# One tile's output product moved a few steps back in a hand-written order, in a retention and phase-MLP kernel on one core

## The chip, the core and the metric

The kernel runs as one program on one core of a Trainium2 chip. The metric is device microseconds of one launch. Five engines run side by side and meet only at semaphores: PE (matrix products; its weight loads are listed apart as PEld), DVE, ACT and POOL (elementwise work), and SP, which here only issues DMAs. Each engine takes its own instructions strictly in the order in which the program emits them, so an instruction that waits holds up all that is behind it on that engine.

## The reference

Two stages follow each other. The first is a retention recurrence over batch 4, 8 heads, 768 positions and head size 64:

```python
gamma = 1.0 - 2.0 ** (-5.0 - np.arange(H))
for t in range(S):
    state = gamma * state + einsum('bhd,bhe->bhde', k[:, :, t], v[:, :, t])
    y[:, :, t] = scale * einsum('bhd,bhde->bhe', q[:, :, t], state)
```

Its output, with the heads side by side (x is 4 x 768 x 512), goes through a phase MLP:

```python
theta = x @ w_theta
zr, zi = x * cos(theta), x * sin(theta)
y = einsum('ts,bsd->btd', w_tok_r, zr) + einsum('ts,bsd->btd', w_tok_i, zi)
u = x + y
out = u + maximum(u @ w_ch, 0)
```

## The kernel before, in words

The 768 positions of a batch are six tiles of 128, so there are 24 tiles, numbered 0 to 23. Retention works on 24 units (a batch, 256 positions, half of the heads), also numbered 0 to 23; units 22 and 23 give the two halves of tiles 22 and 23, units 20 and 21 those of tiles 20 and 21.

There is no scheduler. The list `ORDER` (lines 23 to 87) names every step as a token, and the last lines of the kernel run one small function per token, in that order. A token `M.16.3` calls `M(16, 3)`; a last letter v, a, p or s names the engine or the queue (DVE, ACT, POOL, SP). The place of a token in the list therefore sets the place of its instructions on each engine that it uses, and nothing else does. The tokens that matter below:

- `I.n` (line 457) is the state product of unit n: four PE matmuls of the block-diagonal state `sbd` with the queries. `SB.n.g` (line 140 or 138) copies the state into `sbd` before it, and `S0.n` (line 437) updates the state on DVE.
- `Y.n`, `ST.n` and `A.n` (lines 469, 419 and 392) are the other three retention products, 16 small PE matmuls each. `m.n` (line 401) masks what `A.n` gave, on DVE, for `Y.n`. `XA.n.c` (line 487) and `XB.n.c` (line 140 or 138) write the halves of the finished tile `xT`.
- `Ht.C` and `Hh.C` (line 518) are the theta product of tile C, four PE matmuls of 512 columns; `CT.C.w` and `CN.C.w` (line 525) take cosine and sine on ACT, and `z.C` (line 532) multiplies by x.
- `M.t.s` (line 563) is one sixth of the token sum of output tile t: two PE matmuls of 512 columns. `u.t` (line 570) adds x on DVE.
- `Du.t` (line 585) transposes u into `uT` with a DMA from SP; `Dx.C` (line 508) and `Dk.n` (line 374) do the same for x and for queries and keys.
- `Ot.t` and `O.t` (line 593) are the output product of tile t, four PE matmuls of 512 columns on `uT`. `ft.t` and `f.t` (line 599) add u and the rectified product on DVE; `SO.t` stores it.
- `Vs.*` (line 633) and `ta`, `tb`, `tc_` (lines 646 to 653) prepare sums and differences for the last batch, whose token sums `Na`, `Nb`, `Nc` (line 681) use fewer products.

`Ht` and `Ot` take their PSUM from the same two banks (tag "tr"); `M`, `Hh` and `O` take theirs from two others (tag "acc"). `uT` has three buffers and `ot` four.

Constants are allocated in the order in which the functions `const2`, `const1`, `constQ` and so on run. `qsc`, the decay factors of the queries, is 2 x 12 x 2 floats, so 192 bytes of each partition.

Of the kernel before, what the change touches and what calls it, by code (L numbers as in the profile page):

```python
# [15 lines left out]
FT = mybir.dt.float32  # L16
# [52 lines left out]
SB.20.0.a M.14.3 M.14.2 CT.18.0 CT.18.1 I.20 Lq.23.s M.14.5 A.21 u.13 Dk.22 cv.21.p Y.20 ck.23.a Vs.2.1.v  # L69
z.18.v ST.21 S0.21.v Ot.9 SB.21.0.p cv.22.p Ht.19 M.15.5 SB.21.1.a u.14 m.21 M.15.3 M.15.0 XB.20.1.a cq.23.p  # L70
S1.21 Lv.23.s M.16.0 Dx.19 XB.20.0.v ft.9 Du.12 I.21 A.22 Y.21 ST.22 CT.19.1 cv.23.p SO.6.a XA.21.1 M.15.1
CT.19.0 M.15.2 S0.22.v XA.21.0 m.22 SB.22.0.a SB.22.1.a M.15.4 Vs.0.1.p Ot.12 u.15 Ht.21 I.22 M.16.3 CT.21.0
ta.18.v CT.21.1 M.16.5 z.19.v Y.22 ft.12 Dk.23 ST.23 XB.22.1.a S0.23.v A.23 Du.13 Hh.20 Du.14 Dx.20 M.16.4
Ot.13 Vs.1.1.v XB.22.0.a ta.19.p CN.20.0 m.23 CN.20.1 Vs.2.0.v Ot.14 Dx.21 SB.23.0.p Vs.3.1.v SB.23.1.a
tb.19.p I.23 z.21.v M.16.2 Y.23 M.17.2 M.17.0 M.16.1 M.17.4 ft.13 XA.23.0 XA.23.1 Dx.22 Ht.22 Dx.23 u.16
z.20.v Na.9.1 CT.22.0 CT.22.1 ta.21.v Hh.23 CN.23.0 Du.15 M.17.3 ta.20.v M.17.1 tb.18.v Na.9.0 tb.20.p
Na.10.2 Na.10.1 tc_.20.v tb.21.v z.22.v Na.10.0 CN.23.1 SO.9.a M.17.5 Na.9.3 z.23.v ta.22.v tb.22.v ta.23.v
SO.13.a tc_.18.v Na.10.3 Du.16 Na.10.4 tb.23.v Na.9.2 tc_.23.p Na.9.4 Na.9.5 Na.10.5 u.17 c1.9 g1.9 Ot.15
O.16 e5.9 cx.9.p Du.17 SO.12.s SO.8.a c1.10 g1.10 ft.15 gx.9.p Nb.9.0 e5.10 Nb.9.2 ex.9.v Nb.9.5 Nb.9.1
Nb.9.3 Nb.9.4 f.16 Nb.10.1 tc_.19.v uc.9 Nb.10.3 ub.9 Ot.17 Nb.10.5 Nb.10.4 tc_.22.p ex.10.v ua.9 Nc.9.0  # L80
gx.10.p Na.11.4 Nb.10.2 Nb.10.0 Nc.9.5 cx.10.v tc_.21.p Na.11.1 ft.14 Nc.9.3 ft.17 Nc.9.4 Na.11.3 uc.10
Nc.9.1 Nc.9.2 Na.11.5 Du.18 ub.10 ud.9 Na.11.2 Na.11.0 Nc.10.1 Nc.10.2 SO.15.a Nc.10.5 c1.11 ua.10 e5.11
Nc.10.3 g1.11 O.18 f.18 SO.17.s Nc.10.0 Du.21 gx.11.v Du.19 SO.14.a Nc.10.4 Nb.11.1 SO.16.s ud.10 Nb.11.3
Nb.11.5 Nb.11.2 ex.11.v Nb.11.4 Nb.11.0 ub.11 O.21 ua.11 f.21 uc.11 Tu.20 O.19 Du.22 Nc.11.4 SO.18.s Nc.11.3
Nc.11.2 Eu.20.v Nc.11.1 cx.11.v Nc.11.0 Tuh.1 Nc.11.5 ud.11 SO.21.a O.22 Euh.1 Tuh.0 Euh.0 O.20 f.19 Oh.0
SO.19.s Oh.1 f.22 f.20 fh.0 SO.22.a SO.20.s fh.1 Z.31 SOh.1 SOh.0
""".split()


# [11 lines left out]
def kernel(  # L101
# [16 lines left out]
    P = 128  # L118
    nT = S // P
    nD = dm // P  # L120
    nI = nT // 2
# [6 lines left out]
    const = ctx.enter_context(tc.tile_pool(name="const", bufs=1))  # L128
# [64 lines left out]
    K = {}  # L193

    def const1():
        zero = const.tile([P, dm], BF, name="zero")
        nc.vector.memset(zero, 0.0)
        K["zero"] = zero
        K["sbd"] = [[const.tile([P, 2, 2, P], BF, name=f"sbd{h}{x}") for x in range(2)]
                    for h in range(2)]  # L200
        K["wth"] = const.tile([P, nD, dm], BF, name="wth")
        K["wch"] = const.tile([P, nD, dm], BF, name="wch")
        K["wT"] = [const.tile([P, nT, S], BF, name="wtr"),
                   const.tile([P, nT, S], BF, name="wti")]
        K["row"] = [[const.tile([P, hi - lo, S], BF, name=f"row{r}{lo}")
                     for lo, hi in groups] for r in range(2)]
# [58 lines left out]
                                 bias=K["lscale"], scale=K["lgp"][:, x:x + 1])  # L265

    def const3():
        K["qsc"] = const.tile([P, 2, nI * 4, 2], FT, name="qsc")
        K["vsc"] = const.tile([P, nI, 2, H], FT, name="vsc")
        nc.scalar.activation(K["vsc"].rearrange("p i a h -> p (i a) h"), K["arg"], AF.Exp,  # L270
                             bias=K["zerob"], scale=-1.0)
        K["qx"] = const.tile([P, H // 2, S], FT, name="qx")
# [501 lines left out]
    CT, ft = CN, f  # L774
# [32 lines left out]
```

## Time and profile before

| | |
|---|---|
| time, median of 3 runs | 165.76 us (165.52 to 166.09) |
| the profiled execution's own time | 166.06 us |
| its span, first to last instruction | 164.3 us |
| around the span | 1.76 us |
| granted TensorE clock, mean | 0.999 |

Busy time of the engines in the span: DVE 128.3 us, ACT 82.7 us, POOL 80.9 us; PE is discussed in the prediction. The view of stretches gives, for a window of time, how long each engine was busy; the view of waits gives for an instruction that sat idle what it waited for; the chain of waits follows the run back from its last instruction. In a timeline row the columns are start in us, length in us, engine, source line, operation, output<-input, size and count; brackets give the idle time before it and what ended it. Consecutive matmuls overlap, so the pace of PE is read from start to start and not from their lengths.

### The profile page before, as it was taken

The page shows a single profiled execution, that of the slowest core. Times are in us where ns is not written, and L with a number is a line of the kernel's source. Part 1 is how long each engine was busy: PE and PEld are TensorE (multiplying, and loading weights), DVE is VectorE, ACT ScalarE, POOL GpSimd, SP SyncE. Part 2 cuts the span into 40 slices and gives each one's busy share as a digit, 9 for nine tenths or more (in the row PEclk, how much of TensorE's full clock was granted, in tenths as well). Part 3 has the DMA queues.
Part 4 walks back from the last instruction along what each step waited for, and adds up shares of the span by engine and source line. Part 5 has one row for each costly group of instructions (what it writes and reads, how often), then busy time and mean ns, then how long its engine had stood idle before and what let it go on. Part 6 is the DMA issues. An engine that isn't in the chain of part 4 may idle for free.

```text
span 164.3 us, 5075 instructions
## 1 busy us (share of the span) xinstructions
PE 154.5 (94%) x2072; PEld 90.4 (55%) x2072; DVE 128.3 (78%) x254; ACT 82.7 (50%) x151; POOL 80.9 (49%) x115
## 2 busy tenths in 40 slices
PE   5997889999999999999999999999995999999992
PEld 1354655656666655654555565544552446678650
DVE  5499687977994895994779895887889688796782
ACT  4967798984657245772333724933641715100010
POOL 7797189087214823730307699939177501440000
PEclk9999999999999999999999999999999999999999
DMA  4999999999999998959999896999999306633846
GB/s 131 321 311 227 302 321 237 270 221 218 202 238 138 308 224 186 328 111 284 347 250 199 200 219 198 227 191 291 171 249 124 66 15 144 186 138 97 224 166 221
DMA packets 62919, 34.93 MB, mean 213 GB/s; under 512 B 26416, under 2 KB 59952, under 8 KB 62896
## 3 DMA queue, kind: packets, MB, share of 16 engines
q1 hardware_dynamic: 51680, 23.73, 67.1%
q10 hardware_dynamic: 8528, 7.47, 15.1%
q0 software_dynamic: 2688, 3.41, 12.1%
q8 instruction: 16, 0.26, 0.7%
q14 instruction: 7, 0.06, 0.1%
HBM read 25.69 MB, written 6.29 MB: 195 GB/s over the span
## 4 chain that ended last, share of the span: by engine, by line
PE 72%; DMA 9%; DVE 6%; POOL 5%; issue 3%; ACT 2%; SPq 0%; DVEq 0%; POOLq 0%
PE y_ps L563 26%; PE o_ps L593 11%; PE th_ps L518 9%; DMA row<-in_moe_w_tok_r_dram 6%; PE r_ps L469 3%; PE xw L681 3%; DMA uT<-u 3%; PE kq_ps L358 3%; PE xwv L681 3%; PE vv L681 2%; PE at_ps L392 2%; PE w_ps L540 2%; PE r_ps L457 2%; PE r_ps L419 1%; DVE kqb L344 1%
## 5 line engine op out<-in xcount | busy, mean ns | idle before, releaser
L563 PE MATMUL y_ps<-z,wtr 128*128 128x512 bf16 x108 | 41.0, 380 | 0.0
L563 PE MATMUL y_ps<-z,wti 128*128 128x512 bf16 x108 | 40.9, 379 | 0.0
L350 POOL TENSOR_TENSOR vb<-vf,vsc 128x512 bf16<-128x512 f32 x18 | 19.0, 1057 | 21.3 <-DMA vf<-in_v_dram 14.6
L401 DVE TENSOR_TENSOR at<-at_ps,mask 128x1024 bf16<-128x1024 f32 x24 | 29.2, 1216 | 0.1
L593 PE MATMUL o_ps<-wch,uT 128*128 128x512 bf16 x92 | 23.3, 380 | 1.7 <-DMA uT<-u 1.7
L518 PE MATMUL th_ps<-wth,xT 128*128 128x512 bf16 x96 | 24.7, 379 | 0.1
L525 ACT ACTIVATE cs<-th_ps,halfpi 128x512 bf16<-128x512 f32 x24 | 16.4, 685 | 12.9 <-PE th_ps L518 4.9
L532 POOL TENSOR_TENSOR z<-cs,x_sb 128x1024 bf16<-128x1024 bf16 x8 | 17.0, 2124 | 9.0 <-DVE z L532 4.7
L525 ACT ACTIVATE cs<-th_ps,zerob 128x512 bf16<-128x512 f32 x24 | 16.4, 684 | 7.6 <-PE th_ps L518 7.5
L138 ACT COPY kqT<-kq_ps 128x1024 bf16<-128x1024 bf16 x12 | 12.1, 1012 | 11.8 <-PE kq_ps L358 11.8
L140 POOL CAST sbd<-s 64x256 bf16<-64x256 f32 (+1 forms) x17 | 8.9, 525 | 18.3 <-DVE s L437 17.0
L570 DVE TENSOR_TENSOR u<-y_ps,x_sb 128x512 bf16<-128x512 f32 x18 | 12.4, 686 | 7.1 <-PE y_ps L563 6.9
L599 DVE SCALAR_TENSOR_TENSOR ot<-o_ps,u 128x512 f32<-128x512 f32 x23 | 15.6, 685 | 2.1 <-PE o_ps L593 2.1
L563 PEld LDWEIGHTS <-wtr 128*128 128x128 bf16 x108 | 10.5, 97 | 9.7
L563 PEld LDWEIGHTS <-wti 128*128 128x128 bf16 x108 | 10.6, 98 | 8.8 <-DVE wti L140 0.2
L593 PEld LDWEIGHTS <-uT 128*128 128x128 bf16 x92 | 8.3, 98 | 9.7 <-DMA uT<-u 2.2
L518 PEld LDWEIGHTS <-xT 128*128 128x128 bf16 x96 | 8.8, 98 | 8.3
L138 ACT CAST sbd<-s 64x256 bf16<-64x256 f32 (+1 forms) x24 | 8.9, 372 | 8.3 <-DVE s L437 6.5
L313 PE MATMUL zz<-zero 128*128 128x512 bf16 x30 | 10.3, 479 | 1.9 <-DVE part L232 1.9
L358 PE MATMUL kq_ps<-ident,kqb 128*128 128x128 bf16 x120 | 11.1, 220 | 0.9 <-ACT kqb L138 0.7
L532 DVE TENSOR_TENSOR z<-cs,x_sb 128x1024 bf16<-128x1024 bf16 x16 | 10.9, 686 | 1.1 <-DMA x_sb<-xT 0.9
L138 ACT CAST kqb<-kqf 128x512 bf16<-128x512 f32 x17 | 10.3, 620 | 2.2 <-DMA kqf<-in_k_dram 2.2
(127 smaller groups left out, 276.9 us busy)
## 6 DMA issues: line engine op xcount, KB each, us to landing
vf<-in_v_dram SPq DMA_DIRECT2D x20, 256.0 KB, 5.5
kqf<-in_k_dram SPq DMA_DIRECT2D x19, 256.0 KB, 5.0
kqf<-in_q_dram SPq DMA_DIRECT2D x17, 256.0 KB, 5.3
out_dram<-ot ACTq DMA_DIRECT2D x12, 256.0 KB, 3.1
out_dram<-ot SPq DMA_DIRECT2D x11, 256.0 KB, 3.7
kqf<-in_q_dram ACTq DMA_DIRECT2D x7, 256.0 KB, 5.0
kqf<-in_k_dram ACTq DMA_DIRECT2D x5, 256.0 KB, 5.8
vf<-in_v_dram ACTq DMA_DIRECT2D x4, 256.0 KB, 6.4
```

The source lines that it names most:

```text
L138: nc.scalar.copy(dst, src)
L350: engines[e].tensor_mul(in_blocks(vb), by_token(raw["vf", n]), _bcast_last(K["vsc"][:, i, :, h * HU:(h + 1) * HU], D))
L358: nc.tensor.transpose(st["kq_ps", n][:, 4 * w + x, :], st["kqb", n][:, w, x * P:(x + 1) * P], K["ident"])
L401: nc.vector.tensor_mul(at.rearrange("p g j a t -> p (g j) (a t)"), st["at_ps", n].rearrange("p g j a t -> p (g j) (a t)"), _bcast_mid(K["m ...
L518: nc.tensor.matmul(th_ps, st["xT", C][:, j, :], K["wth"][:, j, :], start=(j == 0), stop=(j == 3))
L525: nc.scalar.activation(st["cs", C][:, w, :], st["th_ps", C], AF.Sin, bias=K["zerob" if w else "halfpi"], scale=1.0)
L532: engines[e].tensor_mul(st["z", b][:, c], st["cs", C], _bcast_mid(x_of(C), 2))
L563: nc.tensor.matmul(st["y", t], K["wT"][r][:, s0, t0 * P:(t0 + 1) * P], st["z", b][:, s0, r, :], start=(done == 0 and r == 0), stop=(done = ...
L570: nc.vector.tensor_add(st["u", t], st["y", t], st["x", b][:, t0, :])
L593: nc.tensor.matmul(o_ps, st["uT", t][:, j, :], K["wch"][:, j, :], start=(j == 0), stop=(j == nD - 1))
L599: nc.vector.scalar_tensor_tensor(st["ot", t], st["o", t], 0.0, st["u", t], ALU.max, ALU.add)
L681: nc.tensor.matmul(o, a, m_, start=(phase == 0 and n == 0 and k != 1), stop=n == nT - 1, skip_group_check=True)
```

## The change

Two tokens are put elsewhere in `ORDER`, and one allocation is made earlier. `Ot.12` stood ahead of `u.15`; it now stands behind `M.16.5`, so behind `Ht.21`, `I.22`, `M.16.3` and `M.16.5`. `ft.12` stood behind `Y.22`; it now stands between `z.19.v` and `Y.22`.

```diff
-... M.15.4 Vs.0.1.p Ot.12 u.15 Ht.21 I.22 M.16.3 CT.21.0
-ta.18.v CT.21.1 M.16.5 z.19.v Y.22 ft.12 Dk.23 ST.23 ...
+... M.15.4 Vs.0.1.p u.15 Ht.21 I.22 M.16.3 CT.21.0
+ta.18.v CT.21.1 M.16.5 Ot.12 z.19.v ft.12 Y.22 Dk.23 ST.23 ...
...
     def const1():
+        K["qsc"] = const.tile([P, 2, nI * 4, 2], FT, name="qsc")
         zero = const.tile([P, dm], BF, name="zero")
...
     def const3():
-        K["qsc"] = const.tile([P, 2, nI * 4, 2], FT, name="qsc")
         K["vsc"] = const.tile([P, nI, 2, H], FT, name="vsc")
```

On PE, behind the last matmul of `M.15.4` (the line 563 row at the top), these are the first rows of each step up to `Y.22` (line 469). A name with a number behind it after "waits" is a semaphore: DMAHW is a DMA's, the others an engine's. Before:

```order
L563 MATMUL y_ps<-z,wti 128x512
L593 LDWEIGHTS uT [waits DMAHW7_49]
L593 MATMUL o_ps<-wch,uT 128x512 [waits DVE_49]
...
L518 LDWEIGHTS xT
L518 MATMUL th_ps<-wth,xT 128x512 [waits Activation_49]
...
L457 LDWEIGHTS sbd_96 [waits DVE_49,Activation_49]
...
L563 MATMUL y_ps<-z,wtr 128x512
...
L469 MATMUL r_ps<-at,vb 64x128 [waits DVE_49]
```

And now, from the same row on:

```order
L563 MATMUL y_ps<-z,wti 128x512
L518 LDWEIGHTS xT
L518 MATMUL th_ps<-wth,xT 128x512 [waits DVE_49]
...
L518 LDWEIGHTS xT [waits DVE_49]
...
L457 LDWEIGHTS sbd_97 [waits DVE_49,Activation_49]
...
L563 MATMUL y_ps<-z,wtr 128x512
...
L593 LDWEIGHTS uT [waits DMAHW7_49]
L593 MATMUL o_ps<-wch,uT 128x512
...
L469 MATMUL r_ps<-at,vb 64x128 [waits DVE_49]
```

The eight instructions of `Ot.12` stand behind 24 others that were behind them. `Ht.21` now takes the PSUM bank that `ft.9` read last (a wait on DVE), and `Ot.12` the one that `CT.19` read last.

On DVE, from `u.15` (line 570) over `ta.18`, `z.19` and `ft.12` (line 599) to `S0.23` (line 437), `Vs.1.1` (line 633) and `m.23` (line 401), the rows of the change are:

```order
L570 TENSOR_TENSOR u<-y_ps,x_sb 128x512 [waits DMAHW2_49,DVE_49,PE_49]
L646 TENSOR_TENSOR zs<-z 128x512
L532 TENSOR_TENSOR z<-cs,x_sb 128x1024 [waits DMAHW6_49,Activation_49]
L599 SCALAR_TENSOR_TENSOR ot<-o_ps,u 128x512 [waits DMAHW2_49,PE_49]
L437 TENSOR_TENSOR s_2780<-r_ps,s_2780 128x128 [waits PE_49]
L633 TENSOR_TENSOR row_109<-row_106,wtr 128x1536 [waits DMASW5_49,Pool_49]
L401 TENSOR_TENSOR at<-at_ps,mask 128x1024 [waits PE_49]
```

Nothing moved there: before, the same rows stand in the same order (`Y.22`, past which `ft.12` was written, has no DVE instruction). ACT, POOL and SP keep their order too. The earlier `qsc` puts every constant from `zero` to `mask` (the states `sbd`, the weights `wth`, `wch`, `wtr`, `wti` and their raw rows among them) 192 bytes further along in its partition and adds no instruction.

More of the change, by code (lines that the diff above doesn't have):

```diff
@@ L71 @@
 S1.21 Lv.23.s M.16.0 Dx.19 XB.20.0.v ft.9 Du.12 I.21 A.22 Y.21 ST.22 CT.19.1 cv.23.p SO.6.a XA.21.1 M.15.1
[L72 to L85, printed above, removed]
@@ L86 @@
-SO.19.s Oh.1 f.22 f.20 fh.0 SO.22.a SO.20.s fh.1 Z.31 SOh.1 SOh.0
+CT.19.0 M.15.2 S0.22.v XA.21.0 m.22 SB.22.0.a SB.22.1.a M.15.4 Vs.0.1.p u.15 Ht.21 I.22 M.16.3 CT.21.0
+ta.18.v CT.21.1 M.16.5 Ot.12 z.19.v ft.12 Y.22 Dk.23 ST.23 XB.22.1.a S0.23.v A.23 Du.13 Hh.20 Du.14 Dx.20
+M.16.4 Ot.13 Vs.1.1.v XB.22.0.a ta.19.p CN.20.0 m.23 CN.20.1 Vs.2.0.v Ot.14 Dx.21 SB.23.0.p Vs.3.1.v
+SB.23.1.a tb.19.p I.23 z.21.v M.16.2 Y.23 M.17.2 M.17.0 M.16.1 M.17.4 ft.13 XA.23.0 XA.23.1 Dx.22 Ht.22
+Dx.23 u.16 z.20.v Na.9.1 CT.22.0 CT.22.1 ta.21.v Hh.23 CN.23.0 Du.15 M.17.3 ta.20.v M.17.1 tb.18.v Na.9.0
@@ new lines @@
+tb.20.p Na.10.2 Na.10.1 tc_.20.v tb.21.v z.22.v Na.10.0 CN.23.1 SO.9.a M.17.5 Na.9.3 z.23.v ta.22.v tb.22.v
+ta.23.v SO.13.a tc_.18.v Na.10.3 Du.16 Na.10.4 tb.23.v Na.9.2 tc_.23.p Na.9.4 Na.9.5 Na.10.5 u.17 c1.9 g1.9
+Ot.15 O.16 e5.9 cx.9.p Du.17 SO.12.s SO.8.a c1.10 g1.10 ft.15 gx.9.p Nb.9.0 e5.10 Nb.9.2 ex.9.v Nb.9.5
+Nb.9.1 Nb.9.3 Nb.9.4 f.16 Nb.10.1 tc_.19.v uc.9 Nb.10.3 ub.9 Ot.17 Nb.10.5 Nb.10.4 tc_.22.p ex.10.v ua.9
+Nc.9.0 gx.10.p Na.11.4 Nb.10.2 Nb.10.0 Nc.9.5 cx.10.v tc_.21.p Na.11.1 ft.14 Nc.9.3 ft.17 Nc.9.4 Na.11.3
@@ new lines @@
+uc.10 Nc.9.1 Nc.9.2 Na.11.5 Du.18 ub.10 ud.9 Na.11.2 Na.11.0 Nc.10.1 Nc.10.2 SO.15.a Nc.10.5 c1.11 ua.10
+e5.11 Nc.10.3 g1.11 O.18 f.18 SO.17.s Nc.10.0 Du.21 gx.11.v Du.19 SO.14.a Nc.10.4 Nb.11.1 SO.16.s ud.10
+Nb.11.3 Nb.11.5 Nb.11.2 ex.11.v Nb.11.4 Nb.11.0 ub.11 O.21 ua.11 f.21 uc.11 Tu.20 O.19 Du.22 Nc.11.4 SO.18.s
+Nc.11.3 Nc.11.2 Eu.20.v Nc.11.1 cx.11.v Nc.11.0 Tuh.1 Nc.11.5 ud.11 SO.21.a O.22 Euh.1 Tuh.0 Euh.0 O.20 f.19
+Oh.0 SO.19.s Oh.1 f.22 f.20 fh.0 SO.22.a SO.20.s fh.1 Z.31 SOh.1 SOh.0
```

## The prediction

> **What bounds the kernel now.** I read the page's first part, then the waits of PE, then the chain of waits, and last the timelines of all engines between 118 and 136 us, where the change lies.
>
> ```profile
> PE 154.5 (94%) x2072; PEld 90.4 (55%) x2072; DVE 128.3 (78%) x254; ACT 82.7 (50%) x151; POOL 80.9 (49%) x115
> PE o_ps L593 <- DMA uT<-u: 1.7, 1, 1.7
> ```
>
> PE is busy for 94% of the span, and the waits of PE hold only one entry of more than a microsecond once the kernel has started: a single output product waits 1.7 us for a transposed u. The chain of waits goes through that very place:
>
> ```profile
> 120.24 5.13 DMA uT<-u
> ...
> 125.42 1.04 PE o_ps L593 x4
> ```
>
> The transpose issued at 120.24 lands 5.13 us later, at 125.37, and 0.05 us after that the product starts; from there the chain goes on over PE. So the end of the run hangs on this landing, and what PE does in the meantime decides what the landing costs. Around it, PE's timeline reads:
>
> ```profile
> 123.34 0.38 PE L563 MATMUL y_ps<-z,wti 128*128 128x512 bf16 x1
> 125.42 1.04 PE L593 MATMUL o_ps<-wch,uT 128*128 128x512 bf16 x4 [1.69 <-DMA uT<-u]
> 126.29 1.03 PE L518 MATMUL th_ps<-wth,xT 128*128 128x512 bf16 x4
> 127.15 0.39 PE L457 MATMUL r_ps<-kqT,sbd 128*128 128x128 bf16 x4
> 127.38 0.38 PE L563 MATMUL y_ps<-z,wtr 128*128 128x512 bf16 x1
> ...
> 128.03 0.38 PE L563 MATMUL y_ps<-z,wti 128*128 128x512 bf16 x1
> 128.34 0.42 PE L469 MATMUL r_ps<-at,vb 64*64 64x128 bf16 x16
> ```
>
> The row at 125.42 is `Ot.12`; behind it stand `Ht.21`, `I.22`, `M.16.3` with `M.16.5`, and `Y.22`. From 127.38 to 128.03 three matmuls of 512 columns pass, 0.217 us each. The last one ahead of the wait starts at 123.34, so the next could have started at 123.56. It starts at 125.42: **1.86 us** of PE's pace are lost (the 1.69 of the bracket counts from the modelled end).
>
> **The change, step by step.** Nothing is computed less or more; one product trades places with the work behind it. `Ht.21` takes 127.15 - 126.29 = 0.86 us, `I.22` 127.38 - 127.15 = 0.23, the two token sums four steps of 0.217 = 0.87, together 1.96. If none of them waits, `Ht.21` starts at 123.56, `I.22` at 124.42, the sums at 124.65, and `Ot.12` at 123.56 + 1.96 = 125.52, against the 125.42 at which its operand lets it start. The wait is covered by 0.10 us, `Y.22` follows 1.86 us sooner than before, and the 1.96 us of work is the most that can ever be gained. Can the steps put ahead start that early?
>
> ```profile
> 120.99 0.68 DVE L599 SCALAR_TENSOR_TENSOR ot<-o_ps,u 128x512 f32<-128x512 f32 x1
> 122.41 0.42 DVE L487 TENSOR_TENSOR xT<-r_ps,qx 128x256 bf16<-128x256 f32 x1 [0.74 <-PE r_ps L419]
> ...
> 123.28 1.21 DVE L401 TENSOR_TENSOR at<-at_ps,mask 128x1024 bf16<-128x1024 f32 x1
> 123.07 0.82 ACT L138 CAST sbd<-s 64x256 bf16<-64x256 f32 x2 [2.03 <-DVE s L437]
> ```
>
> `Ht.21` needs its bank from `ft.9`, free at 121.67, and the half of `xT` from `XA.21.1`, there at 122.83. `I.22` needs both copies into `sbd`, done at 123.89, and banks whose last readers stand ahead of the DVE row of 123.28: 0.53 us to spare. The two sums continue a bank that is already being filled, from products made earlier. So the new head of PE's queue waits for nothing. `Y.22` needs the masked tile of 123.28, ready at 124.49; now it comes at about 126.5.
>
> Next is what comes late when PE runs 1.86 us ahead. The transposes on SP do not move: they are issued back to back and wait for nothing on PE here.
>
> ```profile
> 128.71 0.40 PE L392 MATMUL at_ps<-kqT 64*64 64x128 bf16 x16
> 121.64 1.42 SPq L374 DMA_TRANSPOSE kqT<-kqb  x1
> DMA to landing us min/median/max: 4.6/4.6/4.6
> 127.59 1.22 SPq L508 DMA_TRANSPOSE x_sb<-xT  x1
> DMA to landing us min/median/max: 2.4/2.4/2.4
> 132.47 0.68 DVE L532 TENSOR_TENSOR z<-cs,x_sb 128x1024 bf16<-128x1024 bf16 x1
> ```
>
> `A.23` would start at 128.71 - 1.86 = 126.85, and its `kqT` lands at 121.64 + 4.6 = 126.24: 0.6 us to spare. `z.21` would start at about 130.8 (next paragraph), and its x lands at 127.59 + 2.4 = 130.0.
>
> DVE keeps its order, but not all of it can follow.
>
> ```profile
> 126.09 0.68 DVE L532 TENSOR_TENSOR z<-cs,x_sb 128x1024 bf16<-128x1024 bf16 x1
> 126.69 0.68 DVE L599 SCALAR_TENSOR_TENSOR ot<-o_ps,u 128x512 f32<-128x512 f32 x1
> 128.93 0.29 DVE L437 TENSOR_TENSOR s<-r_ps,s 128x128 f32<-128x128 f32 x1 [1.56 <-PE r_ps L419]
> 129.14 0.95 DVE L633 TENSOR_TENSOR row<-row,wtr 128x1536 bf16<-128x1536 bf16 x1
> 133.68 0.74 DVE L487 TENSOR_TENSOR xT<-r_ps,qx 128x256 bf16<-128x256 f32 x2
> 134.92 0.69 DVE L570 TENSOR_TENSOR u<-y_ps,x_sb 128x512 bf16<-128x512 f32 x1 [0.50 <-PE y_ps L563]
> 130.00:134.00 4.00, 3.92 (x36) 1.71 (x35) 4.00 (x7) 1.67 (x3) 0.97 (x2) 1.00 0.01 2
> ```
>
> `z.19` and `ft.12` do not move: `Ot.12` now ends at 125.52 + 1.04 = 126.56, just ahead of the 126.69 at which DVE is free for `ft.12`. `S0.23` then starts behind it at about 127.3 instead of 128.93, a gain of only 1.63. From there to the end of `XA.23` at 134.42 DVE has no gap (4.00 of 4.00 us busy in that stretch), so this block moves by 1.63; then it idled 0.50 for PE at `u.16`. Being 0.23 slower than PE, it still idles 0.27 there, and from `u.16` on both move by 1.86.
>
> ```profile
> 131.77 0.40 ACT L138 CAST sbd<-s 64x256 bf16<-64x256 f32 x1
> 132.31 0.39 PE L457 MATMUL r_ps<-kqT,sbd 128*128 128x128 bf16 x4
> ```
>
> `I.23` waits before and after for the copy that ends at 132.17 on ACT; that copy stands behind the sine of `Hh.20`, a PE product, so it moves along. Behind 134 us the chain of waits is PE, short answers from DVE, and transposes whose inputs come from PE; I find no row there tied to a time that does not move.
>
> **The address of the constants** moves by 192 bytes (3 x 64). No row of before shows it, so I bound it by the nearest ones.
>
> ```profile
> row<-in_moe_w_tok_r_dram POOLq DMA_DIRECT2D x1, 384.0 KB, 9.3
> row<-in_moe_w_tok_i_dram POOLq DMA_DIRECT2D x1, 384.0 KB, 7.9
> PEld L540 <- DMA row<-in_moe_w_tok_r_dram: 0.6, 1, 0.6
> L563 PE MATMUL y_ps<-z,wtr 128*128 128x512 bf16 x108 | 41.0, 380 | 0.0
> L593 PE MATMUL o_ps<-wch,uT 128*128 128x512 bf16 x92 | 23.3, 380 | 1.7 <-DMA uT<-u 1.7
> ```
>
> A matmul takes 380 ns whether it streams `z`, whose place stays, or `wch`, one of the shifted constants, so for compute I take nothing. A load into the raw rows is on the chain early on; two of equal size differ by 1.4 us. If it landed sooner, PE could gain no more than the 0.6 it waits there; if later, it could lose those 1.4. I take 0, since bytes and order are the same, and keep -0.6 and +1.4 for the range.
>
> **Sum.** The profiled execution took 166.06 us (164.3 of span, 1.76 around it); less 1.86 it would take 164.20. It lies 0.30 above the median of the three runs, 165.76, which becomes **163.90**.
>
> **Rivals.**
>
> First, *DVE and POOL collide and part of the gain stays behind.* One of five equal subtractions on DVE took 1155 ns where the median is 419:
>
> ```profile
> L646 DVE TENSOR_TENSOR zs<-z x5: 417/419/1155, 125.0 to 140.0; 128x512 bf16<-128x512 bf16 x5
> 125.01 1.16 DVE L646 TENSOR_TENSOR zs<-z 128x512 bf16<-128x512 bf16 x1
> 122.80 3.09 POOL L633 TENSOR_TENSOR row<-wtr,wti 128x1536 bf16<-128x1536 bf16 x1
> 126.85 1.16 POOL L646 TENSOR_TENSOR zs<-z 128x512 bf16<-128x512 bf16 x1 [0.96 <-DVE z L532]
> 129.28 1.05 POOL L140 CAST sbd<-s 64x256 bf16<-64x256 f32 x1 [1.28 <-DVE s L437]
> ```
>
> It is the one of 125.01, and it began while POOL was in a `Vs` step that lasted until 125.89; POOL's copy at 129.28 took 1.05 us beside DVE's `Vs.1.1` of 129.14, against the 0.40 of such a copy on ACT. After the change `Vs.1.1` would start at 127.5, inside POOL's subtraction of 126.85 to 128.01. If it blocks until 128.01, DVE loses 0.51, of which the 0.27 at `u.16` is free: 0.24 is left over. If all 0.51 gets through, the gain is 1.35 and the time 164.41. The Trainium skill, "SBUF — State Buffer", section "Who interferes with whom", states this as a rule: a DVE instruction with two SBUF inputs and a GpSimd instruction that reads SBUF exclude each other, and the second waits for the whole of the first. By that rule, with which both rows agree, the collision is certain, and the sum would be 163.90 if the slack takes it and at most 164.41. Also here: the 5.13 us landing may have been longer than usual, but the profiled run is only 0.54 above the fastest of three (165.52), so no more than that of the 1.86 can be its own. Chance 0.14, time about 164.4.
>
> Second, *another wait takes the place of the old one, and nothing is won.* DVE is the candidate: beside that collision it would have to lose another 1.6 us between `S0.23` and `u.16`, with PE held at `Ht.22`, the product that needs `XA.23`. The full stretch of 130 to 134 speaks for it; against it stands that none of its inputs lands late. Time 163.90 + 0.24 + 1.6 = 165.7, chance 0.09.
>
> Third, *slower, through the constants' addresses.* If the shifted row loads landed later, the chain, which passes through one of them, would grow by as much. It gets slower than before by more than 0.3% (0.5 us, about what a measurement of this kernel tells from no change) only from 1.86 + 0.50 = 2.36 us on, a quarter of the 9.3 us landing. At 2.8, twice the difference of equal loads, the time is 163.90 + 2.8 = 166.7. The equal matmul rows speak against any effect of the place. Chance 0.05.
>
> **How the numbers follow.** The forecast has 0.72 with 163.9. The range takes in both ends of the address term, 163.9 - 0.6 = 163.3 and 163.9 + 1.4 = 165.3, which also holds the first rival; about 0.14 is left out. Faster by over 0.3%: 0.72 + 0.14 = 0.86; within it 0.09; slower 0.05.
>
> **What would show it.** Right: PE's wait of 1.7 us for `uT` is gone, `Ht.21` starts near 123.6 and `Ot.12` near 125.5, `S0.23` on DVE near 127.3, `I.23` near 130.5, and all that follows lies about 1.9 us earlier. The first rival shows as a long `Vs.1.1` or a `u.16` that no longer waits for PE; the second as a new wait of PE between 126 and 140; the third as a row load that lands later than the 9.3 us of before. I am wrong if a start before 123 us moves, or if PE's new wait is longer than a few tenths of a microsecond.

## The result, and the profile after

| | before | changed |
|---|---|---|
| median of 14 runs, side by side on one chip | 165.97 us | 164.15 us |
| lowest and highest of these | 164.57 to 173.68 | 164.03 to 164.69 |
| profiled execution, and its span | 166.06, 164.3 | 164.45, 162.7 |
| ratio of the times, with its 95% interval | | 0.9903 (0.9884 to 0.9922) |

The changed kernel is faster by 1.0% (0.8 to 1.2%). The medians differ by 1.82 us, the profiled executions by 1.61, and its runs are spread far less. (Here and below, the ratio and its interval leave out the runs that fell in a slow state, of the 14 of before those of 168.32 and 173.68, so the ratio is not the quotient of the medians.) The page of the changed kernel and its waits of PE, all that were listed between 20 and 165 us:

```profile
PE 152.1 (93%) x2043; PEld 90.8 (56%) x2072; DVE 128.4 (79%) x254; ACT 82.8 (51%) x151; POOL 80.7 (50%) x115
PE y_ps L563 <- issue: 1.1, 7, 0.2
PE r_ps L469 <- DVE at L401: 0.5, 1, 0.5
PE r_ps L457 <- ACT xT L138: 0.4, 1, 0.4
PE x_ps L501 <- ACT kqT L138: 0.2, 1, 0.2
PE o_ps L593 <- DMA out_dram<-ot: 0.2, 1, 0.2
PE o_ps L593 <- issue: 0.2, 1, 0.2
PE vv L681 <- DVE u L737: 0.2, 1, 0.2
```

The wait for `uT` is gone and no wait of its size has come in its place. (29 matmul records are missing from this trace, 2043 of 2072, so PE's busy time is too low by as much; the "issue" entries are where a record is missing or an instruction was late in being dispatched.) PE's timeline at the place of the change, with the last step ahead of it and `I.23` far behind it:

```profile
123.53 0.38 PE L563 MATMUL y_ps<-z,wti 128*128 128x512 bf16 x1
123.75 1.03 PE L518 MATMUL th_ps<-wth,xT 128*128 128x512 bf16 x4
124.61 0.40 PE L457 MATMUL r_ps<-kqT,sbd 128*128 128x128 bf16 x4
124.84 0.38 PE L563 MATMUL y_ps<-z,wtr 128*128 128x512 bf16 x1
...
125.70 1.03 PE L593 MATMUL o_ps<-wch,uT 128*128 128x512 bf16 x4
126.66 0.42 PE L469 MATMUL r_ps<-at,vb 64*64 64x128 bf16 x16
126.91 0.29 PE L419 MATMUL r_ps<-vb,kqb 64*64 64x64 bf16 x16
127.03 0.40 PE L392 MATMUL at_ps<-kqT 64*64 64x128 bf16 x16
...
130.65 0.39 PE L457 MATMUL r_ps<-kqT,sbd 128*128 128x128 bf16 x4
```

`Ht.21`, `I.22` and the two sums follow each other without a gap, then `Ot.12`, `Y.22`, `S0.23`, `A.23`. `I.23` stands at 130.65 instead of 132.31. The clock of events differs from run to run by some tenths before this place is reached, so the sections below compare distances inside a run. The one that sums up the place is from the start of `Ht.21` to `u.16` on DVE:

```profile
126.77 0.69 DVE L599 SCALAR_TENSOR_TENSOR ot<-o_ps,u 128x512 f32<-128x512 f32 x1 [0.51 <-PE o_ps L593]
127.38 0.28 DVE L437 TENSOR_TENSOR s<-r_ps,s 128x128 f32<-128x128 f32 x1
127.58 0.95 DVE L633 TENSOR_TENSOR row<-row,wtr 128x1536 bf16<-128x1536 bf16 x1
...
130.91 0.69 DVE L532 TENSOR_TENSOR z<-cs,x_sb 128x1024 bf16<-128x1024 bf16 x1
...
133.26 0.69 DVE L570 TENSOR_TENSOR u<-y_ps,x_sb 128x512 bf16<-128x512 f32 x1 [0.40 <-PE y_ps L563]
```

It is 133.26 - 123.75 = 9.51 us. In the run of before the last step ahead of the place ended its pace at 123.56, and `u.16` started at 134.92, 11.36 us later. The place has become 1.85 us shorter. It was reached 0.19 us later in this run (123.75, not 123.56), so `u.16` itself comes 1.66 us sooner, and from its start to the end of the span it is 29.4 us in both runs.

One thing, though, does not fit the story of a wait that has been covered, the row of the copy's issue on SP and its landing time:

```profile
119.87 1.24 SPq L585 DMA_TRANSPOSE uT<-u  x1
DMA to landing us min/median/max: 3.8/3.8/3.8
```

In this execution `uT` landed 3.8 us after its issue, at 123.67, and not 5.1 us. The order of before would hardly have waited (its product would have been due at 123.75). So this one profile shows the new order, but not that it was needed; and the landing is not the fixed number that the prediction took it for. The experiments had to settle both.

### The profile page after: what moved, and what is told of

Same layout as the page of the kernel before. It is cut to its first block, busy times and chain, and to the rows that moved or that the text cites. A ratio compares the mean times of both kernels' runs of the same rounds, so it can differ in the third digit from the quotient of the medians.

```text
span 162.7 us, 5046 instructions
## 1 busy us (share of the span) xinstructions
PE 152.1 (93%) x2043; PEld 90.8 (56%) x2072; DVE 128.4 (79%) x254; ACT 82.8 (51%) x151; POOL 80.7 (50%) x115
## 4 chain that ended last, share of the span: by engine, by line
PE 85%; DVE 4%; ACT 4%; issue 2%; DMA 2%; POOL 0%; DVEq 0%; SPq 0%; POOLq 0%
PE y_ps L563 27%; PE th_ps L518 12%; PE o_ps L593 12%; PE zz L313 5%; PE r_ps L469 4%; PE kq_ps L358 4%; PE xw L681 3%; PE at_ps L392 3%; PE xwv L681 3%; PE w_ps L540 3%; PE r_ps L457 3%; PE vv L681 3%; PE x_ps L501 2%; DMA out_dram<-ot 2%; PE r_ps L419 2%
## 5 line engine op out<-in xcount | busy, mean ns | idle before, releaser
L563 PE MATMUL y_ps<-z,wti 128*128 128x512 bf16 x105 | 39.8, 379 | 1.2 <-issue 1.1
L563 PE MATMUL y_ps<-z,wtr 128*128 128x512 bf16 x100 | 37.9, 379 | 0.1
L518 PE MATMUL th_ps<-wth,xT 128*128 128x512 bf16 x88 | 24.2, 379 | 0.6
L593 PE MATMUL o_ps<-wch,uT 128*128 128x512 bf16 x85 | 22.2, 379 | 0.6 <-DMA out_dram<-ot 0.2
L138 ACT CAST xT<-r_ps 128x256 bf16<-128x256 f32 x19 | 6.7, 371 | 9.3 <-PE r_ps L419 8.4
```

The source lines that it names most:

```text
L138: nc.scalar.copy(dst, src)
L518: nc.tensor.matmul(th_ps, st["xT", C][:, j, :], K["wth"][:, j, :], start=(j == 0), stop=(j == 3))
L563: nc.tensor.matmul(st["y", t], K["wT"][r][:, s0, t0 * P:(t0 + 1) * P], st["z", b][:, s0, r, :], start=(done == 0 and r == 0), stop=(done = ...
L593: nc.tensor.matmul(o_ps, st["uT", t][:, j, :], K["wch"][:, j, :], start=(j == 0), stop=(j == nD - 1))
```

## Experiments

Times are medians, each with the ratio to the kernel of before on the same chip. In the expectations tiles are mostly called by their index in the order (the "sixth tile's" store is `SO.6.a`, "nineteenth" is index 19); "the last token sum of the seventeenth tile" is `M.16.5`, which is not the last of that tile's sums in the order.

**1. The two parts of the change apart.** One kernel has the new order alone (`qsc` stays where it was), the other the moved constant alone.

> The two tokens moved, qsc allocated where it was before. If the order makes the gain (my theory), the time is that of the changed kernel, 164.0 to 164.4, and PE does not wait for uT. If the shifted constants make it (rival), for instance by letting the transpose of u land at 3.8 us as in the profile of the changed kernel and not at 5.1, the landing is 5 us again; then Ot.12 still starts without a wait, since 1.96 us of work stand ahead of it, but the time should be a few tenths of a microsecond above 164.4.

> The order of before, only qsc allocated earlier. By my theory the time is that of before, 165.7 to 166.1, and Ot.12 waits 1.5 to 1.9 us for uT. By the rival the transpose lands after about 3.8 us, the wait is near 0 and the time near 164.2.

Measured: order alone 164.07 us (163.97 to 164.57, 9 runs), ratio 0.9907 (0.9876 to 0.9939). Address alone 165.73, ratio 1.0011 (0.9974 to 1.0047). The order makes the gain, and the address makes no difference that shows. With the address alone `Ot.12` waits as before:

```profile
125.01 1.04 PE L593 MATMUL o_ps<-wch,uT 128*128 128x512 bf16 x4 [1.51 <-DMA uT<-u]
```

Rows of the timeline of the order alone, of SP, PE, DVE and POOL in turn, with the landing time of that one copy behind its issue:

```profile
120.39 1.22 SPq L585 DMA_TRANSPOSE uT<-u  x1
DMA to landing us min/median/max: 4.9/4.9/4.9
123.89 1.03 PE L518 MATMUL th_ps<-wth,xT 128*128 128x512 bf16 x4
125.84 1.03 PE L593 MATMUL o_ps<-wch,uT 128*128 128x512 bf16 x4
127.81 1.33 DVE L633 TENSOR_TENSOR row<-row,wtr 128x1536 bf16<-128x1536 bf16 x1
133.40 0.68 DVE L570 TENSOR_TENSOR u<-y_ps,x_sb 128x512 bf16<-128x512 f32 x1
127.17 1.16 POOL L646 TENSOR_TENSOR zs<-z 128x512 bf16<-128x512 bf16 x1 [0.96 <-DVE z L532]
```

This is the profile that the prediction described. `uT` lands late, at 120.39 + 4.9 = 125.29; the order of before would have waited for it from 123.89 on, 1.4 us; and `Ot.12` starts at 125.84 without a wait. It also has the first rival's collision: `Vs.1.1` on DVE starts at 127.81, inside POOL's subtraction of 127.17 to 128.33, and takes 1.33 us instead of 0.95. DVE then has no idle time left ahead of `u.16` (no bracket in its row), and yet `u.16` stands 133.40 - 123.89 = 9.51 us behind `Ht.21`, exactly as in the changed kernel's run without a collision. The slack took all of it. In the changed kernel's run POOL's subtraction ended at 127.49, before `Vs.1.1` began at 127.58:

```profile
126.34 1.15 POOL L646 TENSOR_TENSOR zs<-z 128x512 bf16<-128x512 bf16 x1 [0.97 <-DVE z L532]
```

**2. Half the cover.** The order of before with `Ot.12` moved behind two of the four steps only; `ft.12` not moved.

```
- Vs.0.1.p Ot.12 u.15 Ht.21 I.22 M.16.3 CT.21.0
+ Vs.0.1.p u.15 Ht.21 I.22 Ot.12 M.16.3 CT.21.0
```

> Constants as before; Ot.12 moved back behind Ht.21 and I.22 only, so 0.86 + 0.23 = 1.09 us of work cover the wait instead of 1.96; ft.12 stays where it was. If the gain is the covered part of the wait, it is about 1.1 us: 164.8 to 165.0, with 0.7 to 0.8 us of wait for uT left when the landing is that of before. If the whole gain came from the swap of the two PSUM banks, which this kernel also has, it is 1.8 us and the time 164.1.

Measured: 164.73 us (164.17 to 165.02), ratio 0.9941 (0.9912 to 0.9971), a gain of 1.05 on the 165.78 of before there. Its PE rows:

```profile
123.37 1.03 PE L518 MATMUL th_ps<-wth,xT 128*128 128x512 bf16 x4
124.23 0.39 PE L457 MATMUL r_ps<-kqT,sbd 128*128 128x128 bf16 x4
124.92 1.04 PE L593 MATMUL o_ps<-wch,uT 128*128 128x512 bf16 x4 [0.29 <-DMA uT<-u]
```

The two steps are worth 0.86 + 0.23 = 1.09 us of cover, and the time fell by about as much; the rest of the wait, here 0.29 by the bracket behind a landing of 4.6 us, is still there. The gain goes with the covered part of the wait. The swap of the two PSUM banks, which this kernel has too, did not bring the whole gain.

**3. The landing instead of the order.** The order of before on PE, with the transposed copy of `u` put ahead of the one of x on SP's queue.

```
- Lv.23.s M.16.0 Dx.19 XB.20.0.v ft.9 Du.12 I.21
+ Lv.23.s M.16.0 Du.12 Dx.19 XB.20.0.v ft.9 I.21
```

> Order of PE as before; on SP the transpose Du.12 goes ahead of Dx.19, so it is issued about 1.3 us sooner (near 119.0). If the landing of uT is what PE waits for, the wait shrinks from 1.86 to about 0.5 us and the time is 164.5 to 164.8. If the landing is set by other traffic (the load and the store in flight until about 125) and not by its place in the queue, it lands near 125.4 as before and the time stays at 165.8 to 166.1.

Measured: 164.15 us, ratio 0.9937 (0.9903 to 0.9971), scattered from 163.95 to 165.71. In its profile, one of the fast half (163.95), the copy was issued at 118.89, and `Ot.12` started at 123.30 without a wait, so it had landed after at most 4.4 us:

```profile
118.89 1.21 SPq L585 DMA_TRANSPOSE uT<-u  x1
123.30 1.03 PE L593 MATMUL o_ps<-wch,uT 128*128 128x512 bf16 x4
```

An earlier landing gains what the later reader gains, which shows from the other side that PE waited for nothing else. In size it was a miss: 1.3 us of gain were expected, from an issue 1.3 us sooner with the same 5.1 us behind it, and about half of the runs gained all of it. The landing had become shorter too, which no theory so far explained.

**4. What makes the landing long.** In the profile of before ScalarE's queue issues a 256 KB store, `SO.6.a`, 0.44 us ahead of the copy:

```profile
119.80 0.36 ACTq L604 DMA_DIRECT2D out_dram<-ot  x1
```

It is in flight at the same time (in the changed kernel's profile it landed 3.1 us after its issue). In the order of before it was moved behind `M.16.5`, with all else unchanged.

```
- CT.19.1 cv.23.p SO.6.a XA.21.1 M.15.1
+ CT.19.1 cv.23.p XA.21.1 M.15.1
- ta.18.v CT.21.1 M.16.5 z.19.v Y.22 ft.12
+ ta.18.v CT.21.1 M.16.5 SO.6.a z.19.v Y.22 ft.12
```

> The order of before, with one other edit: the store of the sixth tile's output (256 KB, issued on ScalarE's queue at about 119.8) stands behind the last token sum of the seventeenth tile, so that it no longer is in flight beside the transposed copy of u. Theory A (the landing of 4.6 to 5.1 us after the issue comes from the line of transfers on SyncE's own queue: two loads of 256 KB and two transposed copies ahead of it): landing still 4.6 to 5.1, wait for uT 1.5 to 1.9, time as before, 165.5 to 165.9 us. Rival B (the store is what makes it long): landing down to 3.8 or less, wait at most 0.6, time 164.1 to 164.6.

Measured: 163.94 us, ratio 0.9931 (0.9892 to 0.9971); eight of twelve runs lie at 163.72 to 164.16, the others at 164.52 to 167.01, which I cannot explain. Rows of its timeline, SP's, PE's and ScalarE's queue:

```profile
119.90 1.21 SPq L585 DMA_TRANSPOSE uT<-u  x1
123.28 1.03 PE L593 MATMUL o_ps<-wch,uT 128*128 128x512 bf16 x4
124.15 1.03 PE L518 MATMUL th_ps<-wth,xT 128*128 128x512 bf16 x4
125.32 0.36 ACTq L604 DMA_DIRECT2D out_dram<-ot  x1
```

PE has the order of before and does not wait: `uT` is there within 3.4 us. My own theory, that the line of transfers on SP's queue makes the landing long, fell; the store on the other queue does it (one profile, and the times). The same move in the changed kernel:

> The changed kernel, and in addition the sixth tile's store behind the last token sum of the seventeenth tile, as in the run on the order of before. Theory A (both cover the same wait, which is gone with either): no more than the changed kernel has, 163.8 to 164.2 us, and narrowly spread. Rival B (the two add up): 163.3 or less. Rival C (the later store now delays the last transposed copies of the attention tiles or the next tile's u): 164.4 or more.

Measured: 164.17 us (163.83 to 164.48, 6 runs), ratio 0.9909 (0.9891 to 0.9926), as the changed kernel: either edit removes the same wait, and they do not add up. Its profile gives the landing without the store, 2.5 us, against 3.8 in the changed kernel's own profile and 4.9 with the order alone (issue, landing time, PE's row):

```profile
120.63 1.21 SPq L585 DMA_TRANSPOSE uT<-u  x1
DMA to landing us min/median/max: 2.5/2.5/2.5
125.96 1.03 PE L593 MATMUL o_ps<-wch,uT 128*128 128x512 bf16 x4
```

**5. Does it matter which of the two is issued first?** Two more kernels moved the store by one place on ScalarE's queue, in the order of before and in the new one.

```
- cv.23.p SO.6.a XA.21.1 M.15.1 CT.19.0 M.15.2
+ cv.23.p XA.21.1 M.15.1 CT.19.0 SO.6.a M.15.2
```

> The order of before, with the sixth tile's store one place later on ScalarE's queue, behind the second cosine of the nineteenth tile: issued at about 120.4 to 120.9 instead of 119.8, so behind the transposed copy of u (issued at about 120.2) and still in flight beside it. Theory A (of the two, the one issued second lands late: all profiled runs with the store in front had 4.6 to 5.1 us, the changed kernel's with the copy in front 3.8): landing 3.8 or less, wait at most 0.6, time 163.9 to 164.5. Rival B (the store costs the copy its time whenever both are in flight): landing 4.6 or more, 165.5 to 165.9 us. Rival C (the order of the two issues turns about from run to run, since they lie within 0.6 of one another): times in two groups, near 164.1 and near 165.6.

> The changed kernel with the store one place later on ScalarE's queue. Theory A: uT is no longer waited for in either order, so 163.9 to 164.2, the same as the changed kernel. Rival B (the store now issued behind the copy of u delays the copy of kqT that follows, which S0.23 and A.23 read): S0.23 or A.23 waits 0.3 or more, 164.4 or more.

Measured: in the order of before 165.51 us, ratio 0.9997 (0.9971 to 1.0023), with ten of twelve runs at 165.37 or more and two at 163.70 and 164.26, as the expectation's third rival had it (one of the 17 runs of before beside it, at 164.04, is as fast); in the new order 164.43, ratio 0.9924 (0.9901 to 0.9948). The edit did not do what it was made for: the store was not issued behind the copy. The profiled execution of the first was its fastest run; store and copy are issued together in it (119.56 and 119.58), and `Ot.12` starts at 123.30 without a wait, though the load of its weights waited 0.29 us for `uT`. In the second the store is 0.50 ahead, as the issues, the landing time and PE's row show:

```profile
120.42 0.36 ACTq L604 DMA_DIRECT2D out_dram<-ot  x1
120.92 1.22 SPq L585 DMA_TRANSPOSE uT<-u  x1
DMA to landing us min/median/max: 4.9/4.9/4.9
126.13 1.03 PE L593 MATMUL o_ps<-wch,uT 128*128 128x512 bf16 x4
```

Here `uT` lands at 125.82, and the new order covers it with 0.31 us to spare. Over the profiled executions there is a pattern, though no run forced it. (The kernel with both edits, in section 6, is left out: `uT` is read so late there that its landing is not bounded usefully.) The first column says by how much the store's issue preceded the copy's:

| kernel | store ahead by, us | landing of `uT`, us |
|---|---|---|
| half the cover | 0.66 | 4.6 |
| `Ot.12` behind `A.23` (below) | 0.53 | 4.8 |
| new order, store one place later | 0.50 | 4.9 |
| address alone | 0.49 | 4.9 |
| before | 0.44 | 5.1 |
| order alone | 0.27 | 4.9 |
| order of before, store one place later | 0.02 | at most 3.7 |
| changed kernel | -0.10 | 3.8 |
| copy of `u` first | -0.64 | at most 4.4 |
| store moved away, order of before | none | at most 3.4 |
| store moved away, new order | none | 2.5 |

That the store in flight lengthens the landing is shown by the two kernels that move it away. It does so even when it is not issued first: 3.8 us in the changed kernel, with the store 0.10 behind the copy, against 2.5 without it, one profile each. That it costs more when it is issued clearly ahead fits every row, but stays open.

**6. Further, and both.** The changed kernel with `Ot.12` and `ft.12` moved three steps further, behind `A.23`:

```
- M.16.5 Ot.12 z.19.v ft.12 Y.22 Dk.23 ST.23 XB.22.1.a S0.23.v A.23 Du.13
+ M.16.5 z.19.v Y.22 Dk.23 ST.23 XB.22.1.a S0.23.v A.23 Ot.12 Du.13 ft.12
```

> The changed kernel with the twelfth-index output product moved three steps further, behind Y.22, S0.23 and A.23, and its sum behind the state sum of S0.23. Theory A (PE's order is free here once uT's wait is covered, and what bounds the place is the landing of the last kqT on one side and VectorE's slack of 0.3 to 0.4 ahead of u.16 on the other): A.23 is reached about 0.9 earlier than at 126.66 in the changed kernel's run and waits 0.1 to 0.3 for kqT (landing at 126.1 to 126.2); the sum starts about 0.6 to 1.2 later than at 126.77, VectorE's slack is used up and u.16 comes 0.2 to 0.8 later: 164.2 to 164.9 us. Rival B (neither binds): 164.1, no difference. Rival C (the wait for kqT is as large as the one removed): 165 or more.

(The 126.66 in it is the row of `Y.22`; `A.23` stands at 127.03.) Measured: 164.99 us, ratio 0.9956 (0.9927 to 0.9986), slower than the changed kernel by 0.8 us (they ran on different chips, but the intervals of their ratios do not meet). In its timeline of PE and DVE:

```profile
125.84 0.42 PE L392 MATMUL at_ps<-kqT 64*64 64x128 bf16 x16
127.27 0.69 DVE L599 SCALAR_TENSOR_TENSOR ot<-o_ps,u 128x512 f32<-128x512 f32 x1 [0.55 <-PE o_ps L593]
127.88 1.64 DVE L633 TENSOR_TENSOR row<-row,wtr 128x1536 bf16<-128x1536 bf16 x1
...
133.78 0.68 DVE L570 TENSOR_TENSOR u<-y_ps,x_sb 128x512 bf16<-128x512 f32 x1
```

PE loses about 0.1 us at `A.23` (it starts 0.23 behind the row of `ST.23` at 125.61, elsewhere 0.12), so `kqT` hardly matters. DVE is what binds: it idles 0.55 for the later product with no other work in its order, and `Vs.1.1` behind it takes 1.64. With `Ht.21` at 123.31, `u.16` comes 10.47 us later instead of 9.51. Those 0.96 us are enough for the 0.8.

The changed kernel with the copy of `u` issued first as well:

> The changed kernel, and in addition the transposed copy of u issued ahead of the copy of the nineteenth tile's x_sb, as in the run before. Theory A (the output product's wait for uT was the whole gain, and it is gone already): uT lands 2 us or more ahead of its reader, nothing is left to gain, 163.9 to 164.3 us, the same as the changed kernel within 0.3%. Rival B (the later copy of x_sb is now waited for, since z.19 reads it): z.19 starts up to 0.7 later, which moves the DVE chain, up to 164.8. Rival C (two covers add up, because uT or another landing still binds in many runs): 163.5 or less.

Measured: 164.60 us (164.04 to 165.46), ratio 0.9952 (0.992 to 0.9984); five runs lie at 164.04 to 164.17, as the changed kernel. The profiled execution is one of these (`Ht.21` at 123.51, `u.16` at 133.03, 9.52 us apart), so it does not tell what made the others slower. That two covers do not add up holds; why this version is less even than the changed kernel stays open. None of these kernels is measurably better than the changed one.

## Why the prediction was right

- **The wait is the term.** 1.86 us were to go. The new order alone gives the whole gain, half the cover gives its 1.05 us of it, and two ways of landing `uT` sooner give it without the new order, in most or about half of their runs. The distance from `Ht.21` to `u.16` fell by 1.85 us, the medians by 1.82, the profiled executions by 1.61. The forecast of 163.90 is 0.25 below the measured 164.15; of that, 0.21 is the median of before, which was 165.97 beside it and not 165.76.
- **The cover by a hair.** It was to hold with 0.10 us to spare. In the profiles with a late landing the spare was 0.31 (store one place later) and 0.55 us (order alone), since the landing was 4.9 and not 5.13; with the order alone the copy was also issued sooner, 3.50 us ahead of `Ht.21` and not 3.32.
- **The price downstream.** The sums on DVE were to come later by less than the slack ahead of `u.16`; all from there on was to move by the full 1.86. `u.16` did, measured from `Ht.21`. `I.23`, forecast near 130.5, came at 130.65, and `z.21`, forecast at 130.8, at 130.91.
- **The address at nothing.** Shown by the run with the address alone, within 0.5%.
- **The first rival's mechanism was real, its effect was not.** The collision was there with the order alone (1.33 us instead of 0.95) but not in the changed kernel's profiled run, so it was not certain: there DVE's own subtraction at 125.20 took 0.46 us and not 1.16, and POOL's followed sooner and ended at 127.49, just ahead of the DVE row at 127.58. In the order alone the collision took 0.38 us of DVE and not 0.51, and the slack absorbed it. By the Trainium skill's rule in "SBUF — State Buffer", section "Who interferes with whom", the second instruction is blocked for the whole of the first. The trace agrees that `Vs.1.1`, begun inside POOL's subtraction, was held up, but not in the size: 0.52 us of the subtraction were left, and 0.38 were lost. In the two rows that the prediction took to agree it was 0.74 of 0.88 and 0.66 of 0.81.
- **What the reasoning had wrong without paying for it.** It treated the landing of 5.13 us as belonging to the transpose, and bounded a chance excess by 0.54. It belongs to the company of the store: the same copy took 2.5 us without it, and in the changed kernel's profile, with it, 3.8, which is 1.3 less than in the profile of before. A few runs of before (5 of 32 beside the first four experiments, 164.18 to 164.50) were as fast as the changed kernel, and all its runs lie close together. This is what one would see if the landing were at times short: the old order passes it on to the time, the new one does not. No profile of such a run of before was taken, so this is argued, not shown.
- **One sign against itself could not be read.** The prediction was to be wrong if a start before 123 us moved. Starts there did move: the copy's issue from 120.24 to 119.87, the theta product at 118.65 to 118.83. But with the same instructions ahead of them such starts differ as much from run to run (the copy's issue is at 120.39 with the order alone, 120.27 with half the cover), so a few tenths there tell nothing.

## What to carry to other kernels

Where PE waits for a landing, price the move by the smaller of the wait and the work put ahead, and then look for the first engine behind it whose order cannot follow; here DVE had room for this move and none for one three steps longer. Before reordering the reader, look at what else is in flight when the transfer is issued: moving one store away was worth as much as moving the product. And take a landing time as a spread over several executions, not as a constant. The changed order also made the time repeatable (164.03 to 164.69), though cover alone does not promise that: with the copy issued first as well, the runs scattered from 164.04 to 165.46.

## What the runs showed of the hardware

- One transposed copy of 128 x 512 bf16 landed after 2.5 us with no store beside it, after 3.8 us with a 256 KB store issued 0.10 us behind it on another engine's queue, and after 4.6 to 5.1 us with the store issued 0.27 to 0.66 us ahead. In these runs the two queues were not independent.
- Moving a store by one place behind an activation on ScalarE's queue did not move its issue behind that of the copy on SP: 119.56 against 119.58 in one profile, 120.42 against 120.92 in the other. In the first the activation itself began only at 120.09.
- The DVE step `Vs.1.1` (128 x 1536) took 0.95 us where it began ahead of a POOL copy, which then took 1.05 us and not 0.39, and 1.05 to 1.64 us where it began inside a POOL instruction. It lost a little less than was left of that one: 0.38 of 0.52 us (order alone), 0.33 of 0.47 (half the cover), 0.10 of 0.23 (order of before, store one place later).
